# Attention and two feed-forward layers in one kernel: in blocks 3 and 4 a head pair's values stand behind the transposes of a later row

## The chip, the cores and the metric

The kernel runs on one core of a Trainium2 chip. A core has TensorE (PE in the profile, with its weight loads as PEld), VectorE (DVE), ScalarE (ACT), GpSimd (POOL) and SyncE (SP, which issues the DMAs). Each engine works through its own list of instructions in order; semaphores make one engine wait for another. The metric is the device time of one execution in microseconds (us); less is better.

## The reference

Windowed causal attention, followed by two feed-forward layers, all in float32:

```python
scores = scale * np.matmul(q, k.transpose(0, 1, 3, 2))       # B, H, S, D = 4, 8, 576, 64
mask = (rel >= 0) & (rel < window)                            # window = 128
scores = np.where(mask, scores + bias[None], -1000000000.0)
attn = np.exp(scores - np.max(scores, axis=-1, keepdims=True))
attn = attn / (np.sum(attn, axis=-1, keepdims=True) + 1e-09)
x = np.matmul(attn, v)                                        # to 2304 tokens x 512
h = x @ w_in; g = h * (1.0 / (1.0 + np.exp(-1.702 * h)))      # 512 -> 2048
x = g @ w_out                                                 # 2048 -> 512
g = x @ w_gate; val = x @ w_val                               # 512 -> 1536
out = (g * sigmoid(g) * val) @ w_out2                         # 1536 -> 512
```

## The kernel before

**Blocks.** The 2304 tokens are 18 tiles of 128, in five blocks of 4, 2, 4, 4 and 4 tiles (`A_BLOCKS`). Each block j goes through attention and then through the first feed-forward layer. That layer runs over 16 slices f of its hidden width. `h_part(j, f)` makes one slice: 12 products into one PSUM bank `hp` (each float32 product is made of three, high by high, high by low and low by high), then tanh on ACT into `th` (L719), a step on DVE that reads `hp` for the last time (L721), the high part `gh` on ACT (L727) and the low part `gl` on DVE (L729). `y_part(j, f)`, two slices later, adds the slice to the block's result: 12 products into four banks `y`. "Products" below means these.

**Attention beside it.** While block j-1 is in its feed-forward layer, block j's attention is worked off in small pieces between the products. A head pair has two halves, so eight of each of the first two pieces and four of the third make a block:

- S (`scores_and_norm`): q by k into two banks `sb`, one for each head of the pair. The 16 matmuls take the two banks in turn, beginning with the second head's; they work on quarters of the array (64x64). Then DVE and ACT make the softmax, and POOL scales it.
- T (`transposed`): four transposes on TensorE into one bank `pt` (L554), then `apart`: ACT copies `pt` into the tile `pf` (L585) and POOL cuts it in two (L587, L590). `pf` has one buffer: it is written anew when the values of the pair before have read it.
- V (`values_and_x`): 48 matmuls on quarters of the array, from `pf` and v into two banks `xb` (L388), then `take_x`: ACT copies the first bank into `half` (L675), DVE adds it to the second (L676), ACT takes the high part `xh` (L677) and DVE the low part `xl` (L669).

**What sets the order.** For blocks 3 and 4 the list `PLACES` says at which place of the feed-forward layer a piece is traced: place 2i stands behind `h_part` of slice i, place 2i+1 behind `y_part`. `tc.issue_after` on `marks["h"]` and `marks["y"]` keeps the pieces behind the products that were traced before them, and the same call in `three` keeps the next products behind the last S and V. Inside these limits a scheduler puts each engine's instructions in order when the kernel is built.

**PSUM.** All of this shares eight banks, handed out as they come free: four are held by `y`, so `hp`, `sb`, `pt` and `xb` share the other four. A tile gets a bank whose former owner has been read for the last time, and its first matmul waits for that read.

**Beside it.** ACT and DVE also prepare the weights of the second layer in these blocks (`prepare`, `fraction`, `halves`: the tiles `raw`, `cs`, `wa`, `wb`, lines L253 to L263 and L299), a few steps behind each `h_part` and each `y_part` (`PACE`).

Of the kernel before, what the change touches and what calls it, by code (L numbers as in the profile page):

```python
# [78 lines left out]

LENGTHS = {1: 8, 2: 18}  # L80

JOINED = 3, 4

PLACES = (
    "", "S0", "", "S1", "", "", "", "T0 S2", "", "T1 S3", "", "V0", "", "T2 S4", "", "T3 S5", "", "V1",
    "", "T4 S6", "", "T5 S7", "", "V2", "", "T6", "", "T7", "", "V3", "", "",
)

QUARTERS = 1, 2

# [7 lines left out]
def attention_two_ffn(ctx: ExitStack, tc: tile.TileContext, q, k, v, w_in, w_out, w_gate, w_val, w_out2, yscr, wscr, woscr, out):  # L98
# [41 lines left out]
    def bank(name):  # L140
        return ps.tile([P, 512], F32, tag="b", name=name)
# [174 lines left out]
    units, wides = {}, []  # L316

    def is_wide(j, g):

        return j == 0 and g == 0  # L320

    def blocks_of(i):
        return range(1 if i == 0 else 0, 2)

    def fill(t, n):

        for _ in range(n):
            nc.tensor.matmul(out=t[:, :P], lhsT=ident, rhs=ident, start=True, stop=True)

    def span(j):  # L330

        t0, n = a_blocks[j]
        return t0, n, 0 if kind(t0) == "first" else 1

    def load_pair(j, hp):

        t0, n, lead = span(j)
        qr = att.tile([P, TMAX * P], F32, tag="qr", name="qr", bufs=2)
        kr = att.tile([P, (TMAX + 1) * P], F32, tag="kr", name="kr", bufs=2)
        vr = att.tile([P, 2, TMAX + 1, D], F32, tag="vr", name="vr", bufs=2)  # L340
        rows = slice(hp * P, (hp + 1) * P)
        nc.sync.dma_start(out=qr[:, : n * P], in_=q[rows, t0 * P : (t0 + n) * P])
        nc.sync.dma_start(out=kr[:, : (n + lead) * P], in_=k[rows, (t0 - lead) * P : (t0 + n) * P])
        for e in range(2):
            nc.sync.dma_start(out=vr[:, e, : n + lead, :], in_=v[2 * hp + e, :, t0 - lead : t0 + n, :])
        units[j, hp] = {"q": qr, "k": kr, "v": [vr[:, e] for e in range(2)]}
# [32 lines left out]
    def tiles_of(j, g):  # L379

        return range(2 * g, min(2 * g + 2, a_blocks[j][1]))
# [113 lines left out]
    def reciprocals(j, hp, g):  # L495
        m = 2 * len(tiles_of(j, g))
        prob, stat = units[j, hp]["prob", g]
        nc.vector.tensor_scalar(out=stat[:, 2, :m], in0=stat[:, 1, :m], scalar1=1e-9, scalar2=None, op0=ALU.add)
        nc.vector.reciprocal(out=stat[:, 3, :m], in_=stat[:, 2, :m])  # L499
# [33 lines left out]
    def transposes(j, hp, g, fills=0):  # L533


        u = units[j, hp]
        tiles = tiles_of(j, g)
        m = len(tiles)
        prob = u.pop(("prob", g))[0]
        if is_wide(j, g):  # L540
            u["pt", g] = [bank("pt") for _ in range(2)]
            fill(u["pt", g][0], fills)
            for e in range(2):
                for i in tiles:
                    for b in blocks_of(i):
                        to = (2 * i + b) * P
                        nc.tensor.transpose(
                            out=u["pt", g][e][:, to : to + P], in_=prob[e][:, i, b * P : (b + 1) * P], identity=ident
                        )
        else:  # L550
            pt = bank("pt")
            fill(pt, fills)
            for x in range(2 * m):
                nc.tensor.transpose(out=pt[:, x * P : (x + 1) * P], in_=prob[:, x], identity=ident)  # L554
            u["pt", g] = pt
        if "pf" not in u:
            if j > 0:
                u["pf"] = att.tile([P, 4 * TMAX, P], F32, tag="pf", name="pf", bufs=1)
            else:
                u["pf"] = wpool.tile([P, 4 * TMAX, P], F32, tag=f"w{PFS + hp}", name="pf")  # L560

    def apart(j, hp, g, select):

        u = units[j, hp]
        m = len(tiles_of(j, g))
        pt = u["pt", g]
        if is_wide(j, g):
            lo = P * blocks_of(2 * g)[0]
            to = u["pf"][:, 8 * g + 4 * select : 8 * g + 4 * select + 4, :].rearrange("p x c -> p (x c)")
            if (hp, select) in COPY_ON_VECTOR:  # L570
                nc.vector.tensor_copy(out=to[:, lo:], in_=pt[select][:, lo : 4 * P])
            else:
                nc.scalar.activation(out=to[:, lo:], in_=pt[select][:, lo : 4 * P], func=AF.Copy)
            return
        before = u["pf"][:, 8 * g : 8 * g + 4 * m : 2, :]
        own = u["pf"][:, 8 * g + 1 : 8 * g + 4 * m : 2, :]
        src = pt[:, : 2 * m * P].rearrange("p (x c) -> p x c", c=P)

        if (j, hp, g) in ON_VECTOR:
            for out_, mask in ((own, keep), (before, drop)):  # L580
                nc.vector.tensor_tensor(
                    out=out_, in0=src, in1=mask.unsqueeze(1).to_broadcast([P, 2 * m, P]), op=ALU.mult
                )
        elif not select:
            nc.scalar.activation(out=own, in_=src, func=AF.Copy)  # L585
        else:
            nc.gpsimd.affine_select(  # L587
                out=before, in_=own, compare_op=ALU.is_gt, fill=0.0, base=0, pattern=[[0, 2 * m], [-1, P]], channel_multiplier=1
            )
            nc.gpsimd.affine_select(  # L590
                out=own, in_=own, compare_op=ALU.is_ge, fill=0.0, base=0, pattern=[[0, 2 * m], [1, P]], channel_multiplier=-1
            )
# [101 lines left out]
    begun = {}  # L694
# [264 lines left out]
    def scores_and_norm(*u):  # L959
        with tc.issue_after(marks["h"]), tc.issue_after(marks["y"]):  # L960
            scores(*u)
        for e in range(2):
            minima(*u, e)
            exponentials(*u, e)
        reciprocals(*u)
        normalise(*u)

    def transposed(*u):
        if u[0] in JOINED:
            with tc.issue_after(marks["h"]), tc.issue_after(marks["y"]):  # L970
                transposes(*u)
        else:
            transposes(*u)
        for select in range(2):
            apart(*u, select)

# [95 lines left out]
    def hooks(j, length):  # L1072

        ev = []

        G = (a_blocks[j][1] + 1) // 2
        step = 2 * length * SPREAD / (G * H // 2)
        at = 2 * (begin[j] - length)
        lag = TRANSPOSE_LAG if j != 2 else 6.5

        def start():
            load_pair(j, 0)
            load_pair(j, 1)

        if j > 1:
            ev.append((at - 1, start))
        if j in JOINED:
            for n, place in enumerate(PLACES):
                for what in place.split():
                    h = int(what[1:])  # L1090
                    if what[0] == "V":
                        ev.append((at + n, lambda h=h: values_and_x(j, h)))
                        continue
                    u = j, h // G, h % G
                    if what[0] == "T":
                        ev.append((at + n, lambda u=u: transposed(*u)))
                        continue
                    ev.append((at + n, lambda u=u: scores_and_norm(*u)))
                    if h % G == G - 1 and h // G + 2 < H // 2:
                        ev.append((at + n + 1, lambda h=h: load_pair(j, h // G + 2)))  # L1100
            return [(min(p, 2 * begin[j] - 1), e) for p, e in ev]
        begun, scored, valued = 0, 0, []
        for h in range(G * H // 2):
            u = j, h // G, h % G
            scored = max(at + step * h, scored + 1)
            for p in valued:
                if p <= scored < p + APART:
                    scored = p + APART
            ev.append((scored, lambda u=u: scores_and_norm(*u)))
            last = h % G == G - 1  # L1110
            if last and h // G + 2 < H // 2:
                ev.append((at + step * (h + LOAD_LAG), lambda h=h: load_pair(j, h // G + 2)))
            begun = max(begun, at + step * h + lag)
            ev.append((begun, lambda u=u: transposed(*u)))
            if last:
                begun = begun + step * (VALUES_LAG if j != 2 else 1.6)
                valued.append(begun)
                ev.append((begun, lambda u=u: values_and_x(*u[:2])))
        return [(min(p, 2 * begin[j] - 1), e) for p, e in ev]

    ev = []
    for j in range(1, na):
        ev += hooks(j, LENGTHS.get(j, NF1))
# [178 lines left out]
```

## Time and profile before

| | before |
|---|---|
| three timed runs, median (lowest to highest) | 896.36 us (894.97 to 897.86) |
| the profiled execution's own time | 894.27 us |
| its span, from first to last instruction | 892.6 us |
| busy: PE, PEld, DVE, ACT, POOL | 99%, 89%, 75%, 51%, 14% |
| granted TensorE clock over the span | 0.998 |

The profile is of one execution; its own time is 1.67 us more than its span. In a timeline row the first number is the start and the second the duration. Matmuls are pipelined, so a row's duration overlaps the next row: what a piece costs TensorE is read from the distance between starts.

### The profile page before, as it was taken

To read this page: it belongs to the slowest core of one execution; us is meant where nothing else is said; L and a number is where in the kernel's file an instruction comes from. 1 tells how busy PE (TensorE), PEld (TensorE's weight loads), DVE (VectorE), ACT (ScalarE), POOL (GpSimd) and SP (SyncE) were. 2 spreads that over 40 slices of the span, in tenths; PEclk is the share of its full clock that TensorE was granted. 3 is DMA by queue.
4 is the path that set the end of the run, shared out by engine and by line. 5 is a ranking of instruction groups with operands and counts; after the bars stand their busy time and mean duration, and the time that the engine had idled before them with its cause. 6 is when DMAs were issued, how large, how long until landed. Compare 5 with 4: busy or idle time off the path is not lost.

```text
span 892.6 us, 15625 instructions
## 1 busy us (share of the span) xinstructions
PE 883.8 (99%) x5556; PEld 792.8 (89%) x5556; DVE 672.0 (75%) x1707; ACT 455.7 (51%) x1065; POOL 121.7 (14%) x218
## 2 busy tenths in 40 slices
PE   8999999999999999999999999999999999999998
PEld 6787779997778777788888999999999999999998
DVE  8988847758886788776757486779866779766777
ACT  6866646646555566554445364335344345344331
POOL 6401424403242123210000000000000000000000
PEclk9999999999999999999999999999999999999999
DMA  9961214435565575556864587787887787887664
GB/s 324 385 258 30 72 57 147 142 119 188 186 208 179 205 244 200 199 184 217 272 246 170 180 310 264 252 310 263 285 289 258 254 309 269 288 296 256 252 217 142
DMA packets 71309, 199.20 MB, mean 223 GB/s; under 512 B 6720, under 2 KB 37952, under 8 KB 64320
## 3 DMA queue, kind: packets, MB, share of 16 engines
q1 hardware_dynamic: 71232, 198.21, 62.8%
q8 instruction: 44, 0.72, 0.3%
q14 instruction: 33, 0.27, 0.1%
HBM read 155.71 MB, written 42.47 MB: 222 GB/s over the span
## 4 chain that ended last, share of the span: by engine, by line
PE 93%; DVE 5%; POOL 1%; issue 1%; ACT 0%; DVEq 0%; POOLq 0%; ACTq 0%
PE sx L847 17%; PE ox L847 8%; PE sz L847 8%; PE y L684 7%; PE hp L684 7%; PE y L686 7%; PE y L685 7%; PE hp L685 7%; PE hp L686 7%; PE oz L847 4%; PE sy L847 4%; PE xb L388 2%; PE sb L388 2%; PE oy L847 2%; PE pt L554 1%; DVE cv L228 1%
## 5 line engine op out<-in xcount | busy, mean ns | idle before, releaser
L847 PE MATMUL sx<-ya,wg 128*128 128x384 f32 x864 | 172.4, 335 | 0.0
L847 PEld LDWEIGHTS sx<-ya,wg 128*128 128x128 f32 x864 | 151.9, 188 | 0.1
L684 PE MATMUL hp<-xh,wt 128*128 128x512 f32 (+1 forms) x320 | 121.2, 379 | 0.0
L684 PE MATMUL y<-gh,wt 128*128 128x512 f32 (+1 forms) x320 | 119.3, 376 | 0.0
L685 PE MATMUL hp<-xl,wt 128*128 128x512 f32 (+1 forms) x320 | 118.2, 369 | 0.5 <-DVE xl L669 0.4
L686 PE MATMUL y<-gh,wt 128*128 128x512 f32 (+1 forms) x320 | 117.9, 369 | 0.0
L686 PE MATMUL hp<-xh,wt 128*128 128x512 f32 (+1 forms) x320 | 117.9, 368 | 0.0
L685 PE MATMUL y<-gl,wt 128*128 128x512 f32 (+1 forms) x320 | 117.8, 368 | 0.0
L847 PE MATMUL ox<-p,wg 128*128 128x384 f32 x432 | 89.6, 337 | 0.0
L876 DVE TENSOR_TENSOR p<-th,p 128x384 fp32r<-128x384 f32 x126 | 68.2, 554 | 28.1 <-ACT p L875 27.4
L847 PE MATMUL sz<-ya,wg 128*128 128x384 f32 x432 | 88.8, 336 | 0.0
L729 DVE TENSOR_TENSOR gl<-th,gh 128x512 fp32r<-128x512 f32 (+1 forms) x80 | 52.3, 655 | 39.8 <-ACT gh L727 39.3
L875 ACT ACTIVATE p<-th 128x384 fp32r<-128x384 f32 x126 | 63.5, 521 | 36.3 <-DVE th L871 28.6
L509 POOL TENSOR_SCALAR prob<-prob,stat 128x128 f32<-128x128 f32 x112 | 56.8, 525 | 183.0 <-DVE stat L499 116.3
L847 PEld LDWEIGHTS ox<-p,wg 128*128 128x128 f32 x432 | 76.5, 188 | 0.0
L847 PEld LDWEIGHTS sz<-ya,wg 128*128 128x128 f32 x432 | 76.1, 188 | 0.1
L727 ACT ACTIVATE gh<-th 128x512 fp32r<-128x512 f32 (+1 forms) x80 | 46.9, 586 | 53.3 <-PE y L686 27.4
L882 ACT ACTIVATE th<-c 128x384 f32<-128x384 f32 x54 | 28.3, 525 | 86.9 <-DVE c L867 86.7
L684 PEld LDWEIGHTS y<-gh,wt 128*128 128x128 f32 x320 | 60.2, 188 | 13.7 <-issue 2.9
L684 PEld LDWEIGHTS hp<-xh,wt 128*128 128x128 f32 x320 | 60.1, 188 | 13.6 <-issue 2.7
L685 PEld LDWEIGHTS hp<-xl,wt 128*128 128x128 f32 x320 | 60.2, 188 | 10.7 <-DVE xl L669 1.5
L686 PEld LDWEIGHTS hp<-xh,wt 128*128 128x128 f32 x320 | 60.1, 188 | 10.5 <-DVE wt L238 0.2
(110 smaller groups left out, 1555.6 us busy)
## 6 DMA issues: line engine op xcount, KB each, us to landing
wg<-w_scratch SPq DMA_DIRECT2D x36, 1024.0 KB, 5.1
wg<-w_scratch SPq DMA_DIRECT2D x36, 768.0 KB, 5.0
wg<-wo_scratch SPq DMA_DIRECT2D x18, 1024.0 KB, 6.7
wg<-wo_scratch SPq DMA_DIRECT2D x18, 768.0 KB, 7.5
w_scratch<-wa SPq DMA_DIRECT2D x24, 512.0 KB, 2.7
w_scratch<-wb SPq DMA_DIRECT2D x24, 384.0 KB, 3.3
wraw<-in_moe_w_in SPq DMA_DIRECT2D x16, 512.0 KB, 9.1
wraw<-in_moe_w_out SPq DMA_DIRECT2D x16, 512.0 KB, 9.2
```

The lines of the kernel that those rows point to most:

```text
L228: nc.vector.scalar_tensor_tensor(out=made["c"], in0=made["c"], scalar=3, in1=low, op0=ALU.logical_shift_left, op1=ALU.bitwise_or)
L388: return matmul(**kw).ins
L509: nc.gpsimd.tensor_scalar(out=of[x], in0=of[x], scalar1=stat[:, 3, x : x + 1], scalar2=1.0, op0=ALU.mult, op1=ALU.mult,)
L684: nc.tensor.matmul(out=out_ap, lhsT=whi, rhs=xhi, start=start, stop=False)
L685: nc.tensor.matmul(out=out_ap, lhsT=whi, rhs=xlo, start=False, stop=False)
L686: marks[products] = nc.tensor.matmul(out=out_ap, lhsT=wlo, rhs=xhi, start=False, stop=stop).ins
L727: a = nc.scalar.activation(out=gh[:, :m], in_=th[:, :m], func=AF.Copy)
L729: d = nc.vector.tensor_tensor(out=gl[:, :m], in0=th[:, :m], in1=gh[:, :m].bitcast(F32), op=ALU.subtract)
L847: nc.tensor.matmul(out=bank_[:, :HT], lhsT=w[:, kk, at, a, :], rhs=p2[2 * (q // 2 - 1) + kk, i][:, b, :] if m == "O" else y2[q // NP2, i][ ...
L875: nc.scalar.activation(out=t[:, 0], in_=src, func=AF.Copy)
L876: nc.vector.tensor_tensor(out=t[:, 1], in0=src, in1=t[:, 0].bitcast(F32), op=ALU.subtract)
L882: nc.scalar.activation(out=th, in_=g, func=AF.Tanh, scale=0.5)
```

## The change

The list `PLACES` is written anew for blocks 3 and 4. S and T keep their places. Three of the four V of a block move: V of pair 0 from place 11 to 13, of pair 1 from 17 to 19, of pair 2 from 23 to 25, each behind the T that stands there and, at 13 and 19, ahead of the S that stands there. V of pair 3 stays at 29, alone. `transposed` is cut in two: the transposes come first, then V, then `selected` (the copies of `apart`), then S. `pf` is handed out in `apart` and no longer in `transposes`, since V must have read the old one.

```diff
-JOINED = 3, 4
-
-PLACES = (
-    "", "S0", "", "S1", "", "", "", "T0 S2", "", "T1 S3", "", "V0", "", "T2 S4", "", "T3 S5", "", "V1",
-    "", "T4 S6", "", "T5 S7", "", "V2", "", "T6", "", "T7", "", "V3", "", "",
-)
+PLACES = {
+    3: """
+    | S0 | | S1 | | | | T0 S2 | | T1 S3 | | | | T2 V0 S4 | | T3 S5 | | | | T4 V1 S6 | | T5 S7 | | | | T6 V2 | | T7 | | V3
+    """,
+}
+PLACES[4] = PLACES[3]
...
     def transposed(*u):
-        if u[0] in JOINED:
+        if u[0] in PLACES:
             with tc.issue_after(marks["h"]), tc.issue_after(marks["y"]):
                 transposes(*u)
         else:
             transposes(*u)
+
+    def selected(*u):
         for select in range(2):
             apart(*u, select)
...
-            for n, place in enumerate(PLACES):
+            for n, place in enumerate(PLACES[j].split("|")):
+                late = None
...
                     if what[0] == "T":
                         ev.append((at + n, lambda u=u: transposed(*u)))
+                        late = u
                         continue
+                    if late:
+                        ev.append((at + n, lambda u=late: selected(*u)))
+                        late = None
                     ev.append((at + n, lambda u=u: scores_and_norm(*u)))
```

What this makes of the order on TensorE, at V of pair 0 in block 3. The numbers behind a name are those of the buffer; `xb_2890` and `xb_2891` are the first and the second of V's banks before, `sb_2980` and `sb_2981` the banks of S4. First the order before, from V's end to the first matmuls of S4:

```order
L388 MATMUL xb_2890<-pf_2719,vr_2435 64x64
L684 MATMUL hp_2933<-xh_1826,wt_729 128x512 [waits DVE_49,PE_49]
...
L684 MATMUL y_2650<-gh_2774,wt_704 128x512 [waits Activation_49]
...
L554 MATMUL pt_2971<-ident_70,prob_2733 128x128 [waits DVE_49]
L554 MATMUL pt_2971<-ident_70,prob_2733 128x128 x3
L388 MATMUL sb_2981<-kr_2634,qr_2633 64x192 [waits DMAHW6_49,DMAHW5_49,Activation_49]
L388 MATMUL sb_2980<-kr_2634,qr_2633 64x192 [waits DVE_49]
```

24 products stand between V and S4. In the changed kernel the same place reads as follows; here V's banks are `xb_2943`, the first, and `xb_2944`, and `sb_2980` lies in the bank that `xb_2943` had:

```order
L554 MATMUL pt_2938<-ident_70,prob_2733 128x128 [waits DVE_49,PE_49,Pool_49]
L554 MATMUL pt_2938<-ident_70,prob_2733 128x128 [waits Pool_49] x3
L388 MATMUL xb_2944<-pf_2719,vr_2435 64x64 [waits DVE_49,DMAHW4_49,PE_49,Pool_49]
L388 MATMUL xb_2943<-pf_2719,vr_2435 64x128 [waits DVE_49]
...
L388 MATMUL xb_2943<-pf_2719,vr_2435 64x64
L388 MATMUL sb_2981<-kr_2634,qr_2633 64x192 [waits DMAHW6_49,DMAHW5_49,DVE_49]
L388 MATMUL sb_2980<-kr_2634,qr_2633 64x192 [waits Activation_49]
```

V stands between T2 and S4, and the second matmul of S4 waits for ACT: for the copy `half` of `xb_2943`. The same three pieces stand so at four places: T2 V0 S4 and T4 V1 S6, in both blocks.

On ACT, at V of pair 0 in block 4. Before, `half` stands right behind `gh` of the slice whose `hp` products stand right ahead of V:

```order
L719 ACTIVATE th_4102<-hp_4089 128x512 [waits PE_49]
L253 ACTIVATE cs_4086<-raw_4019 128x512 [waits DMAHW5_49,DMAHW4_49,DVE_49]
L727 ACTIVATE gh_4105<-th_4102 128x512 [waits DVE_49]
L675 ACTIVATE half_4164<-xb_4136 128x512 [waits PE_49,Pool_49]
L262 ACTIVATE wa_4169<-cs_4086 128x2x128 [waits DMAHW2_49,DVE_49,Activation_49]
```

In the changed kernel `half` is the last of a longer list at the same place:

```order
L727 ACTIVATE gh_4105<-th_4102 128x512 [waits DVE_49]
L719 ACTIVATE th_4155<-hp_4142 128x512 [waits PE_49]
L262 ACTIVATE wa_4136<-cs_4086 128x2x128 [waits DMAHW2_49,DVE_49,Activation_49]
L262 ACTIVATE wa_4136<-cs_4086 128x2x128 [waits DVE_49]
L727 ACTIVATE gh_4158<-th_4155 128x512 [waits PE_49]
L262 ACTIVATE wb_4162<-cs_4086 128x3x128 [waits DMAHW1_49,DVE_49]
L253 ACTIVATE cs_4166<-raw_4117 128x512 [waits DMAHW3_49,DMAHW2_49,DVE_49]
L675 ACTIVATE half_4215<-xb_4187 128x512 [waits PE_49,Pool_49]
L585 ACTIVATE pf_4220<-pt_4182 128x4x128 [waits Pool_49]
```

`gh_4158` waits for TensorE there: `gh` has two buffers, and the one it takes is read by the `y` products that stand ahead of T2. Of the list behind it, `wb` and `cs` stand ahead of `half`; `cs` waits for DVE.

## Rows read from the trace of the kernel before

**Rows 1.** Windows, blocks 3 and 4: length, busy us by engine, clock, DMA.

```profile
195.00:300.00 105.00, 105.00 (x743) 84.54 (x742) 81.58 (x262) 60.15 (x159) 30.94 (x48) 1.00 0.55 191
300.00:405.00 105.00, 105.00 (x730) 83.52 (x729) 84.78 (x277) 63.55 (x166) 26.86 (x48) 1.00 0.58 204
```

**Rows 2.** Waits of PE, whole span: total us, times, longest; first of five.

```profile
PE pt L328 <- POOL ident masks.py:199: 1.4, 1, 1.4
```

**Rows 3.** Timeline of PE, block 4, V of pair 1, alone between products.

```profile
353.98 0.39 PE L686 MATMUL y<-gh,wt 128*128 128x512 f32 x1
354.30 1.58 PE L388 MATMUL xb<-pf,vr 64*64 64x64 f32 x48
355.81 0.50 PE L684 MATMUL hp<-xh,wt 128*128 128x512 f32 x1
356.15 0.39 PE L685 MATMUL hp<-xl,wt 128*128 128x512 f32 x1
356.38 0.39 PE L686 MATMUL hp<-xh,wt 128*128 128x512 f32 x1
```

**Rows 4.** Timeline of PE, block 4, T3 and S5 between products.

```profile
347.23 0.60 PE L554 MATMUL pt<-ident,prob 128*128 128x128 f32 x4
347.76 0.88 PE L388 MATMUL sb<-kr,qr 64*64 64x192 f32 x16
348.57 0.50 PE L684 MATMUL y<-gh,wt 128*128 128x512 f32 x1
348.91 0.40 PE L684 MATMUL hp<-xh,wt 128*128 128x512 f32 x1
```

**Rows 5.** Timeline, block 2: V, T behind it, `half`, the addition.

```profile
174.88 1.47 PE L388 MATMUL xb<-pf,vr 64*64 64x128 f32 x48
...
176.28 0.66 PE L554 MATMUL pt<-ident,prob 128*128 128x128 f32 x4
...
176.46 0.60 ACT L675 ACTIVATE half<-xb 128x512 f32<-128x512 f32 x1 [1.03 <-PE xb L388]
...
177.09 0.70 DVE L676 TENSOR_TENSOR xb<-xb,half 128x512 f32<-128x512 f32 x1 [1.21 <-ACT half L675]
```

**Rows 6.** Timeline of PE, block 4, T6 alone between products.

```profile
382.76 0.60 PE L554 MATMUL pt<-ident,prob 128*128 128x128 f32 x4
383.11 0.48 PE L684 MATMUL hp<-xh,wt 128*128 128x512 f32 x1
383.43 0.39 PE L685 MATMUL hp<-xl,wt 128*128 128x512 f32 x1
```

**Rows 7.** Timeline of ACT and DVE at T3 of block 4.

```profile
347.43 0.63 ACT L727 ACTIVATE gh<-th 128x512 fp32r<-128x512 f32 x1 [0.37 <-PE y L686]
...
348.10 0.84 DVE L729 TENSOR_TENSOR gl<-th,gh 128x512 fp32r<-128x512 f32 x1 [0.59 <-ACT gh L727]
...
348.86 0.42 DVE L254 TENSOR_SCALAR raw<-raw 128x512 uint32<-128x512 uint32 x1
```

**Rows 8.** Timeline of ACT and DVE around `half` of V2, block 4.

```profile
378.59 0.69 DVE L256 SCALAR_TENSOR_TENSOR cs<-cs,raw 128x512 uint32<-128x512 uint32 x1
379.31 0.42 ACT L262 ACTIVATE wa<-cs 128x256 fp32r<-128x256 f32 x1 [1.33 <-DVE cs L256]
379.32 0.70 DVE L299 TENSOR_TENSOR cs<-cs 128x128 f32<-128x128 f32 x3
379.64 0.58 ACT L675 ACTIVATE half<-xb 128x512 f32<-128x512 f32 x1
379.93 0.42 DVE L263 TENSOR_TENSOR wa<-cs,wa 128x256 fp32r<-128x256 f32 x1
```

**Rows 9.** Timeline of ACT and DVE around `half` of V1, block 4.

```profile
357.37 0.55 DVE L263 TENSOR_TENSOR wb<-cs,wb 128x384 fp32r<-128x384 f32 x1
...
357.96 0.66 ACT L253 ACTIVATE cs<-raw 128x512 f32<-128x512 f32 x1 [1.71 <-DVE wb L263]
358.52 0.59 ACT L675 ACTIVATE half<-xb 128x512 f32<-128x512 f32 x1
```

More of the change, by code (lines that the diff above doesn't have):

```diff
@@ L555, in transposes, with apart @@
             u["pt", g] = pt
+    def apart(j, hp, g, select):
+        u = units[j, hp]
         if "pf" not in u:
@@ L560, in transposes @@
                 u["pf"] = wpool.tile([P, 4 * TMAX, P], F32, tag=f"w{PFS + hp}", name="pf")
-    def apart(j, hp, g, select):
-        u = units[j, hp]
         m = len(tiles_of(j, g))
@@ L1086, in hooks @@
             ev.append((at - 1, start))
-        if j in JOINED:
-            for n, place in enumerate(PLACES):
+        if j in PLACES:
+            for n, place in enumerate(PLACES[j].split("|")):
+                late = None
                 for what in place.split():
@@ L1100, in hooks @@
                         ev.append((at + n + 1, lambda h=h: load_pair(j, h // G + 2)))
+                if late:
+                    ev.append((at + n, lambda u=late: selected(*u)))
             return [(min(p, 2 * begin[j] - 1), e) for p, e in ev]
@@ L1113, in hooks @@
             begun = max(begun, at + step * h + lag)
-            ev.append((begun, lambda u=u: transposed(*u)))
+            ev.append((begun, lambda u=u: (transposed(*u), selected(*u))))
             if last:
```

## The prediction

> **What bounds the kernel now.** I read first the windows of the two stages that the change touches. TensorE is busy for 105.00 of 105.00 us in each of them, at full granted clock (1.00, so 2.4 GHz), while DVE is busy for 81.58 and 84.78 and ACT for 60.15 and 63.55 [rows 1]. Then the waits of TensorE over the whole span: the longest is 1.4 us, at the start of the program [rows 2], and as the windows are full, none falls into blocks 3 and 4. So there is no wait here for the change to remove. What it can win is time that TensorE spends on passing from one kind of matmul to another; what it can lose is any wait that it puts on TensorE, since nothing but TensorE sets the end there. From there I went to the timeline of TensorE, for the price of a piece between products, and to the timelines of ACT and DVE, for how fast V's results are taken out of PSUM.
>
> **What the change removes: passages.** Products start 0.23 us apart (356.15 to 356.38) [rows 3]. A V that stands alone starts 0.32 us after the last product ahead of it, 0.09 more than that pace; the next product starts 1.51 us after V (354.30 to 355.81); and the one behind comes 0.34 us later, 0.11 more [rows 3]. So V alone costs 0.09 + 1.51 + 0.11 = 1.71 us. T with S behind it costs 0.53 (T to S), 0.81 (S to the next product) and again 0.34 - 0.23 = 0.11: 1.45 us [rows 4]. Together 3.16 us.
>
> With V between them, T to V should cost the 0.53 of T to S, since V and S work on the same quarters. V to S has no row. The nearest is V with T behind it in block 2, with the same 48 matmuls, where T starts 1.40 us after V [rows 5]; I take 1.40. Above it lies the 1.51 of V to a product [rows 3]; below, nothing says that a passage between equal quarters is free, and if the 0.09 of entering quarters were the price of a passage, 1.31. The sum is 0.53 + 1.40 + 0.81 + 0.11 = 2.85 us, so a place of this kind wins 0.31 (0.20 to 0.40). There are four, two in each block: 1.24 us.
>
> The third V that moves stands behind T6 and ahead of products. T6 alone costs 0.35 to the next product and 0.32 - 0.23 = 0.09 behind it, 0.44 us [rows 6]; with V alone 2.15. Together they cost 0.53 + 1.51 + 0.11 = 2.15. It wins nothing.
>
> The Trainium skill ("TensorEngine Tiling (Array Packing)", section Key Properties) says that changing the tiling mode drains TensorE, and changing the tile within a mode does not. The trace agrees: the 0.09 and 0.11 stand at V's edges. By that rule alone the change would win its four passages, the 1.24 us above.
>
> No instruction is added or removed. S and T keep their places, so the loads that are issued behind S keep theirs in SP's queue; the fetches and stores of the weight preparation move by a few rows with it. The POOL cuts of a pair's `pf` have more time than before, since V comes two places later.
>
> **What the change adds: a wait on TensorE.** Ahead, V's banks had 24 products to be emptied in. Now S stands right behind V, and the bank of S's second matmul is the first of V's two banks, free only when ACT has copied `half` from it. S is in order on TensorE, and the next products must follow S, so everything behind stands. Without a wait S's second matmul would start at about 0.53 + 1.40 + 0.05 = 1.98 us after T's start (0.05 is S's 0.81 over 16 matmuls).
>
> The least that the wait can be: in block 2, with ACT idle, `half` starts 0.18 us after V's successor could start, and DVE, which waits for it, starts 0.63 us after `half` (176.46, 177.09) [rows 5]. That frees S at 0.53 + 1.40 + 0.18 + 0.63 = 2.74: a wait of 0.76 us, 3.0 for the four.
>
> But ACT will not be idle. In the changed order `half` stands behind `gh` of the last slice and steps of the weight preparation, and this `gh` waits for the end of the `y` products ahead of T, so the list can't be worked off earlier. The same wait shows now at T3 of block 4: `gh` starts 0.20 us after T, released by a `y` product; `gl` follows on DVE at 0.87, and DVE's next instruction at 1.63 after T's start (347.23, 347.43, 348.10, 348.86) [rows 4, 7]. From there I follow the changed order at each place, in us after T's start:
>
> - Block 3, V0: DVE's step on `cs` (L256) at 1.63; `wa` on ACT 0.72 later, 2.35; `half` 0.33 later, 2.68 [rows 8]; S is free 0.63 later, 3.31. Wait: 3.31 - 1.98 = 1.33.
> - Block 3, V1: the same to `wa`; three subtractions on DVE last 0.70 (3.05), a second `wa`, `half` 0.33 later (3.38) [rows 8], S free at 4.01. Wait: 2.03.
> - Block 4, V0: DVE has `raw` at 1.63, for 0.42 [rows 7]; then `wb`, with `cs` on ACT 0.59 behind its start (2.64) and `half` 0.56 behind that (3.20) [rows 9]; S free at 3.83. Wait: 1.85.
> - Block 4, V1: three subtractions (0.70) and a split of `wa` (0.42) on DVE from 1.63 on, 2.75; `wb`, then `half`, taken at the 0.33 of a `wa` (3.08) [rows 8]; S free at 3.71. Wait: 1.73.
>
> The four make 6.9 us. It can be more: these chains suppose that ACT reaches `gh` when `y` ends. Now `half` of V1 in block 4 starts 2.71 us after V's successor (355.81 to 358.52) [rows 3, 9]; with such a delay S would be free 2.71 + 0.63 = 3.34 us after V's end, a wait of about 3.3 at each place, 13 in all. I take 6.9, between 3.0 and 13, and nearer the lower end, because while TensorE stands ACT and DVE catch up.
>
> The Trainium skill ("Perfetto Trace Analysis", section Matmuls) says that independent groups of matmuls should go through different banks, so that the emptying of one lies beside the matmuls of the next. That speaks against this change: S takes the bank that V has just filled. The trace agrees as far as it goes, since with 24 products between the two TensorE waits nowhere in these blocks.
>
> **Where the stall goes.** Behind S, the next `hp` takes the bank of `pt`, whose copy follows `half` on ACT by one instruction, while 12 `y` products lie between: no second wait. The next T (T3, T5) waits for V's second bank, that is for the addition, `xh` and `xl`: about 0.7 us each (the addition's 0.70 [rows 5]), 2.1 with `half` done, and 24 products of 0.23, 5.5 us, stand between. Covered; if it weren't, it would cost what is missing from 5.5.
>
> **The sum.** -1.24 + 6.9 = +5.7 us on the profiled execution's own 894.27: 900.0 us. That execution lies 2.1 us below the median of the timed runs (896.36). The forecast for the median is 896.36 + 5.7 = 902.1, said as **902 us**.
>
> **The rivals.** A measurement of this kernel can tell about 0.3% from no change, 2.7 us.
>
> - *ACT is ready* (not slower). At all four places `half` follows V at once. Price: 4 x 0.76 - 1.24 = +1.8, 898.2 us, no change that can be told. It decides below an average wait of (2.7 + 1.24) / 4 = 0.98 us. For it: in block 2 `half` waits for V with ACT idle [rows 5]. Against it: the order on ACT, with `cs` or `wa` behind DVE ahead of `half`. Chance 0.16.
> - *Passages alone* (the bank is free in time, so that the wait does nothing and only the four passages count): 896.36 - 1.24 = 895.1, the same again. To be faster by 2.7 us, a place would have to win 0.67, twice what its edges cost now. Against it: S's second matmul reads the bank's release from ACT, and ACT cannot copy before V ends. Chance 0.04, of which 0.02 with a gain above 0.3%. (It is what the rule on modes in the Trainium skill's "TensorEngine Tiling (Array Packing)" would give by itself.)
> - *ACT is late*: tanh of the slice before is held up by the softmax of the last S, `gh` comes late, and each place waits as long as `half` is late now: 13 - 1.24, near +12, 908 us; half of that excess gives 905. For it: the 2.71 us [rows 3, 9]. Against it: that V had `half` behind a `cs` that waited for DVE by 1.71 us [rows 9], on which nobody waited; it is the worst row. Chance 0.14.
> - *The forecast*, waits of 1.0 to 2.4 us at the places, +2.7 to +8 in all: 899.1 to 904.4. Chance 0.66.
>
> So faster 0.02, within 0.3% 0.18, slower 0.80. The range that leaves out no more than 2 in 10 runs from the case where ACT is ready (898.2) to the middle of the case where it is late (906).
>
> **What would show it.** In the waits of TensorE a new row, S's matmul or its weight load (`sb` L388) released by ACT's `half` (L675), four times, near 7 us in all; windows of blocks 3 and 4 in which TensorE is no longer busy throughout; starts from V to S's first matmul near 1.40 us; `half` right behind `wa`, `wa`, `cs` and `wb` in the order of the four places; no wait at the next T; a stage from block 4's end on of the same length as before. The prediction is wrong if TensorE waits elsewhere, for instance at T for POOL or at V for `pf`, or if the four waits are below 1 us.

## The result and the profile after

The changed kernel takes 904.58 us (median of 6, 902.84 to 907.96), the kernel before 897.11 beside it (median of 6, 894.97 to 900.41): ratio 1.0082, 95% interval 1.0060 to 1.0104. By the medians it is slower by 7.5 us. (The ratios here and below are taken over all runs, and differ by up to 0.15% from the quotient of the two medians.) Forecast were 902.0, the range 898.2 to 906.0, and slower with 0.80. The profiled execution took 905.49 us, its span 903.8.

First the waits of TensorE over the whole span (total us, times, longest), which answer to [rows 2]:

```profile
PE sb L388 <- ACT half L675: 5.6, 4, 1.7
PE y L684 <- ACT gh L727: 1.9, 1, 1.9
...
PE y L685 <- DVE gl L729: 0.6, 1, 0.6
```

The first row is the one that the prediction named. The other two belong to one place behind block 4 and were not foreseen. The windows of blocks 3 and 4, against [rows 1]: TensorE is no longer busy throughout.

```profile
195.00:300.00 105.00, 102.60 (x733) 82.86 (x733) 77.82 (x255) 59.28 (x156) 24.12 (x48) 1.00 0.55 191
300.00:405.00 105.00, 101.81 (x716) 81.19 (x715) 82.68 (x272) 60.84 (x160) 25.34 (x48) 1.00 0.56 196
```

One of the four places, T2 V0 S4 of block 4, on the timelines of TensorE, ACT and DVE:

```profile
341.92 0.60 PE L554 MATMUL pt<-ident,prob 128*128 128x128 f32 x4
342.45 1.58 PE L388 MATMUL xb<-pf,vr 64*64 64x64 f32 x48
343.82 0.38 PE L388 MATMUL sb<-kr,qr 64*64 64x128 f32 x2
345.92 0.88 PE L388 MATMUL sb<-kr,qr 64*64 64x128 f32 x14 [1.73 <-ACT half L675]
346.73 0.50 PE L684 MATMUL y<-gh,wt 128*128 128x512 f32 x1
...
342.22 0.42 ACT L262 ACTIVATE wa<-cs 128x256 fp32r<-128x256 f32 x1 [1.07 <-DVE cs L299]
342.54 0.62 ACT L727 ACTIVATE gh<-th 128x512 fp32r<-128x512 f32 x1
343.06 0.51 ACT L262 ACTIVATE wb<-cs 128x384 fp32r<-128x384 f32 x1
344.72 0.66 ACT L253 ACTIVATE cs<-raw 128x512 f32<-128x512 f32 x1 [1.15 <-DVE wb L263]
345.28 0.59 ACT L675 ACTIVATE half<-xb 128x512 f32<-128x512 f32 x1
345.76 0.60 ACT L585 ACTIVATE pf<-pt 128x512 f32<-128x512 f32 x1
...
344.14 0.55 DVE L263 TENSOR_TENSOR wb<-cs,wb 128x384 fp32r<-128x384 f32 x1
```

S begins at 343.82, behind V, and could have gone on. ACT comes to `half` at 345.28 only: `cs` stands ahead of it and waits 1.15 us for DVE's `wb`. S stands from its first pair of rows at 343.82 to 345.92. (The 16 and 48 matmuls that are told of S and V are rows of the trace: the kernel issues 8 and 24, and each leaves two rows. So the pair is S's first matmul, and the second one waits.) At the four places this gap is 1.24, 2.12, 2.10 and 1.84 us, where the prediction took 0.05 as unstalled. (The row of waits counts 5.6, less than these gaps, since it begins where the pair's modelled duration ends.)

From the start of S0 in block 3 to the start of V3 in block 4 TensorE takes 204.50 us (196.67 to 401.17; before 198.83, 195.91 to 394.74): +5.7. The remaining 5.5 us of the span's growth lie outside, 0.8 ahead and 4.8 behind. Most of the latter is here, in block 4's own feed-forward layer:

```profile
466.19 0.84 ACT L783 ACTIVATE ya<-yr 128x768 fp32r<-128x768 f32 x1 [6.55 <-DMA yr<-y_scratch]
...
467.60 0.49 PE L684 MATMUL y<-gh,wt 128*128 128x512 f32 x1 [1.91 <-ACT gh L727]
468.68 0.70 PE L685 MATMUL y<-gl,wt 128*128 128x512 f32 x1 [0.58 <-DVE gl L729]
469.18 0.63 PE L686 MATMUL y<-gh,wt 128*128 128x512 f32 x1
469.60 0.63 PE L684 MATMUL y<-gh,wt 128*128 128x512 f32 x1
```

ACT stands 6.55 us for a read (`ya` is the first step of the second layer's input), `gh` stands behind it, TensorE waits for `gh` and `gl`, and then its products start 0.42 us apart instead of 0.23 for some 3 us. In the profile of before ACT stood 4.88 us for the same read and TensorE did not wait.

### The profile page after: what moved, and what is told of

Same layout as the page of the kernel before. It is cut to its first block, busy times and chain, and to the rows that moved or that the text cites. A ratio compares the mean times of both kernels' runs of the same rounds, so it can differ in the third digit from the quotient of the medians.

```text
span 903.8 us, 15620 instructions
## 1 busy us (share of the span) xinstructions
PE 885.8 (98%) x5556; PEld 794.1 (88%) x5556; DVE 672.1 (74%) x1707; ACT 456.4 (51%) x1065; POOL 113.4 (13%) x218
## 3 DMA queue, kind: packets, MB, share of 16 engines
q1 hardware_dynamic: 71232, 198.21, 62.0%
## 4 chain that ended last, share of the span: by engine, by line
PE 75%; DVE 9%; DMA 8%; ACT 4%; issue 2%; SPq 1%; DVEq 0%; POOL 0%; ACTq 0%; POOLq 0%
PE sx L847 17%; PE ox L847 8%; PE sz L847 8%; PE y L684 5%; PE hp L684 4%; PE y L685 4%; PE y L686 4%; PE hp L685 4%; PE hp L686 4%; PE oz L847 4%; PE sy L847 4%; DMA raw<-in_moe_w_out 2%; PE oy L847 2%; PE sb L388 2%; DMA raw<-in_moe_w_gate 1%
## 5 line engine op out<-in xcount | busy, mean ns | idle before, releaser
L684 PEld LDWEIGHTS y<-gh,wt 128*128 128x128 f32 x320 | 60.6, 189 | 17.6 <-issue 4.5
L509 POOL TENSOR_SCALAR prob<-prob,stat 128x128 f32<-128x128 f32 x112 | 49.4, 459 | 191.3 <-DVE stat L499 108.6
L684 PEld LDWEIGHTS hp<-xh,wt 128*128 128x128 f32 x320 | 60.1, 188 | 12.0 <-issue 1.6
L685 PEld LDWEIGHTS y<-gl,wt 128*128 128x128 f32 x320 | 60.6, 189 | 10.8 <-DVE gl L729 1.1
L686 PEld LDWEIGHTS y<-gh,wt 128*128 128x128 f32 x320 | 60.6, 189 | 10.4
```

Of the source, the lines that this page charges most:

```text
L509: nc.gpsimd.tensor_scalar(out=of[x], in0=of[x], scalar1=stat[:, 3, x : x + 1], scalar2=1.0, op0=ALU.mult, op1=ALU.mult,)
L684: nc.tensor.matmul(out=out_ap, lhsT=whi, rhs=xhi, start=start, stop=False)
L685: nc.tensor.matmul(out=out_ap, lhsT=whi, rhs=xlo, start=False, stop=False)
L686: marks[products] = nc.tensor.matmul(out=out_ap, lhsT=wlo, rhs=xhi, start=False, stop=stop).ins
```

## The experiments

Three theories were put to the test. **A**: S waits for the bank that V has just filled, `half` is late because of what stands ahead of it on ACT, and the passages win a little. **B**: the order itself, V two places later with longer lists on ACT and DVE, costs the time, whatever the bank. **C**: part of the difference is made at the read of `yr` behind block 4, in its strong form by the changed kernel alone, in its weak form in any of these kernels, now and then. A stretch below is always the time on TensorE from S0 of block 3 to V3 of block 4, and the rest what the span has behind V3 (before: 198.83 and 497.86 us). Both are read from the one profiled execution of a kernel; the time given for a kernel is the median of all its runs.

**The change in block 3 alone** (`only3`).

```diff
-PLACES[4] = PLACES[3]
+PLACES[4] = """
+    | S0 | | S1 | | | | T0 S2 | | T1 S3 | | V0 | | T2 S4 | | T3 S5 | | V1 | | T4 S6 | | T5 S7 | | V2 | | T6 | | T7 | | V3
+    """
```

> The change in block 3 alone; block 4 keeps the old list. Theory A (S stands because its second bank is the one that V has just filled, and is free only when ACT has copied half; less the passages won): block 3's two gaps between S's first pair and its other matmuls were 1.24 and 2.12 us in the changed kernel, its two passages win 0.34 each, so +2.7 us against the kernel before, about 900 us, ratio 1.003, with two waits of sb on half and none in block 4; block 4 as before, 105.0 us busy of 105. Theory B (the order itself costs the time, through later V and longer lists on ACT and DVE, not the bank): also about half, so this run does not part A from B. Theory C (a good part of the difference comes after block 4, from the reads of yr that ACT waited for near 455 us): if that follows from the changed order of blocks 3 and 4, some of its 3 to 5 us stays; if it comes and goes by itself, the time is +2.7 whatever that place shows.

898.84 us against 897.15, ratio 1.0013 (0.9990 to 1.0036). Two waits on `half`, 2.4 us in all, both in block 3. Stretch 201.75: +2.9, as A says; B says about the same here.

**S one place later** (`later`). The edit is made for both blocks.

```diff
-T2 V0 S4 | | T3 S5 | | | | T4 V1 S6 | | T5 S7
+T2 V0 | S4 | T3 S5 | | | | T4 V1 | S6 | T5 S7
```

> V as in the changed kernel, but S4 and S6 one place later in both blocks, so that 12 products of hp (2.8 us) stand between V and S. Theory A: the longest gap was 2.1 us behind V, so it is covered by 2.8 us of products; the passage from V to S is lost, the one from T to V stays; 0 us against the kernel before within 1 us, ratio 0.999 to 1.001, no wait of sb on half, or a short one. Theory B (the later V and the longer lists on ACT and DVE cost the time): still slower by 4 us or more, with TensorE waiting elsewhere. Theory C: the wait on yr near 455 us stays if it follows from the later V.

901.46 us, ratio 1.0046 (1.0023 to 1.0068): by the time alone a miss for A, and what B forecast. Theory A was right at three places of four: block 3 takes 91.97 us from S0 to V3, before 92.01. At the fourth, V1 of block 4, V started at 360.99, and still:

```profile
366.69 0.43 DVE L254 TENSOR_SCALAR raw<-raw 128x512 uint32<-128x512 uint32 x1 [2.82 <-DMA raw<-in_moe_w_out]
367.62 0.66 ACT L253 ACTIVATE cs<-raw 128x512 f32<-128x512 f32 x1 [3.58 <-DVE wb L263]
368.19 0.58 ACT L675 ACTIVATE half<-xb 128x512 f32<-128x512 f32 x1
...
368.82 2.04 PE L388 MATMUL sb<-kr,qr 64*64 64x128 f32 x16 [3.30 <-ACT half L675]
370.79 0.79 PE L684 MATMUL y<-gh,wt 128*128 128x512 f32 x1
```

A load of `raw` comes late, DVE stands for it 2.82 us ahead of `wb`, `cs` on ACT waits for `wb`, and `half`, which needs none of this, stands behind `cs`. S waits 3.30 us although 2.8 us of products lie between. S itself then lasts 1.97 us instead of 0.80, and the first products behind it run at the slow pace too. With these the stretch is 204.28, +5.5, all of it in block 4. So the distance of V and S is not all: what stands ahead of `half` decides.

**`half` copied twice** (`twice`).

```diff
-nc.scalar.activation(out=half, in_=x[0][:, :m], func=AF.Copy)
+for _ in range(2 if j > 2 else 1):
+    nc.scalar.activation(out=half, in_=x[0][:, :m], func=AF.Copy)
```

> The changed kernel with half copied twice by ACT in blocks 3 and 4 (the second copy writes the same values again). Theory A: V's first bank comes free one copy later, 0.5 to 0.6 us, at each of four places: +2.2 us over the changed kernel, about +9.5 us against the kernel before, ratio near 1.0105, the four waits of sb on half longer by 0.5 to 0.6 each, and no other wait of TensorE in blocks 3 and 4. Theory B: ACT has spare time, so one more copy of 0.5 us adds nothing that can be seen at these places beyond what the changed kernel has.

911.95 us, ratio 1.0151 (1.0119 to 1.0182): 7.4 more than the changed kernel, where 2.2 were expected. V's bank is held longer, so that S takes the bank of the transposes, whose copy stands behind the first `half`:

```profile
349.82 1.55 PE L388 MATMUL sb<-kr,qr 64*64 64x128 f32 x14 [2.69 <-ACT pf L585]
```

The stretch is 213.25, 8.8 above that of the changed kernel's profile. The four gaps are 1.99, 2.46, 3.07 and 2.55 us, 2.8 more than there, 0.7 on average: about one copy more on ACT, one copy more of waiting. B, by which the copy adds nothing, does not fit. Nearly all of the rest is the clock: behind three of the four gaps S and the products run at about half their pace (products 0.42 to 0.43 us apart instead of 0.23), for 3.6 to 6.2 us each, and that costs 5.9 us in all.

**The transposes' bank copied first** (`early`).

Shortened, and the two comments are not in the kernel:

```diff
+    # in apart, ahead of V: the copy into the tile that the probabilities had
+    nc.scalar.activation(out=u["pc", g][:, : 2 * m], in_=pt, func=AF.Copy)
...
-in_=own
+in_=own_from        # POOL cuts pf from that tile, behind V
```

> The changed kernel's order on TensorE (T V S without products between), but in blocks 3 and 4 ACT copies the transposes' bank right behind T, while V runs, into the tile that the probabilities had (they are used up by then), and POOL cuts pf from there after V. So the bank that is free first is that of the transposes, and S takes it in place of V's first. Theory A: the copy of the transposes ends at 1.3 to 1.9 us after T, S's second matmul could start at 1.95: waits of 0 to 0.5 us at a place, the passages' 0.34 each won: -1.4 to +0.6 us against the kernel before, ratio 0.9985 to 1.0005; no wait of sb on half. Theory B (order, not bank): slower by 4 us or more, as the changed kernel.

901.64 us, ratio 1.0039 (1.0016 to 1.0062), stretch 201.95: +3.1 instead of -1.4 to +0.6. By the time alone (+4.5) this is again what B forecast. No wait on `half`, and two short ones on the copy (0.48 and 0.36 us). But T5 of block 4 waited 0.74 for `xl`, and S7 behind it 0.61 for DVE: the last steps of V's way stand behind the preparation on DVE, which there waited 1.30 us for `raw`. The rest is 502.68, +4.8, with the waits of TensorE for `gh` (1.4) and `gl` (0.6) at the read of `yr` in it, as in the changed kernel. A held for the bank and was incomplete: the engines that empty it were still tied to the loads of the preparation. The next runs take that away.

**The preparation kept away from V** (`calm_mark`, and with the early copy `calm_early_mark`); the control is the kernel before with the same holding (`before_calm`, without the last edit, by which later steps stay behind `half`), and the changed kernel ran once more (`after_again`).

Shortened, with comments that are not in the kernel:

```diff
+    held = {...}        # the two places ahead of T2 V0 S4 and of T4 V1 S6
+    def paced(at, n):
+        if at in held:
+            saved[0] += n
+            return
+        more = min(saved[0], n / 2)
+        saved[0] -= more
+        advance(n + more)
...
-            advance(PACE[j])
+            paced(2 * idx, PACE[j])
...
+            if j in PLACES:
+                marks["x"] = copied        # half: later steps of the preparation stand behind it
```

> The changed kernel with the weight preparation held back at the two places ahead of each T V S and given back afterwards, and with its later steps kept behind half. On ACT half then stands right behind gh at all four places, with no cs, wa or wb between; on TensorE the order and the banks are those of the changed kernel. Theory A (S waits for half, and half is late because it stands behind steps of the preparation, which themselves wait for DVE or for a load): only the floor is left, S's second matmul about 0.8 us behind its first at each of four places; with 0.34 won by each passage that is 4 x (0.76 - 0.34) = +1.7 us against the kernel before, ratio near 1.002, and 5.5 us less than the changed kernel. Theory B (the later V and the longer way of its values cost the time, whatever stands on ACT): as the changed kernel, +7 us.

> The same, and besides ACT copies the bank of the transposes right behind gh, ahead of half, and S's second bank is that one. Theory A: the copy starts about 0.85 us after T and is done 0.6 us later, before V ends at 1.9: no wait at S, the four passages won, and the preparation no longer stands ahead of V's additions, so the wait that the early copy alone had at T5 of block 4 (for xl, 0.74 us, behind a load of raw that DVE waited for) is gone: -1.4 us against the kernel before, ratio 0.997 to 1.001. Theory B: +4 us or more.

> The kernel before with the preparation held back at the same places and given back in the same way, V where it was. A control for the two runs with the preparation held: by theory A it changes nothing on TensorE in blocks 3 and 4 (105.0 us busy of 105), 0 us within 1; if the holding itself costs or wins time, for instance by loads and stores that come later and meet the reads of yr near 455 us, this run shows how much.

> The changed kernel once more, for its ratio beside the others on one chip and for a second look at the place near 467 us. Theory A: ratio 1.008 again, the four waits of sb on half 5.6 us in all within 0.5, 204.5 us from S0 of block 3 to V3 of block 4. Theory C: if the wait of TensorE for gh (1.9 us) and the stretch at 0.42 us a product behind it, in which ACT had stood for the read of yr, belong to the changed kernel, they are there again; if they come and go, this look has another size or none.

| | us | ratio to before (896.86) | stretch | rest |
|---|---|---|---|---|
| `calm_mark` | 903.69 | 1.0065 (1.0041 to 1.0090) | 202.29 | 503.38 |
| `calm_early_mark` | 898.58 | 1.0010 (0.9994 to 1.0027) | 198.21 | 500.35 |
| `before_calm` | 900.82 | 1.0049 (1.0024 to 1.0073) | 199.45 | 503.22 |
| `after_again` | 904.78 | 1.0082 (1.0059 to 1.0105) | 207.02 | 500.31 |

By the time alone `calm_mark` missed (+6.8, not +1.7). The control shows why: holding the preparation back costs 4.0 us by itself, and the profile has it in the rest (+5.4), not in the stretch (+0.6). It is the read of `yr` again:

```profile
461.31 0.84 ACT L783 ACTIVATE ya<-yr 128x768 fp32r<-128x768 f32 x1 [6.17 <-DMA yr<-y_scratch]
...
462.73 0.51 PE L684 MATMUL y<-gh,wt 128*128 128x512 f32 x1 [1.77 <-ACT gh L727]
463.80 0.50 PE L685 MATMUL y<-gl,wt 128*128 128x512 f32 x1 [0.57 <-DVE gl L729]
```

Against the control `calm_mark` is 2.9 us slower and `calm_early_mark` 2.2 faster. Against the kernel before, `calm_early_mark` is 1.7 slower where 1.4 less was forecast, with the ratio in the range that was given. `after_again` repeats the four waits (6.2 us in all, stretch 2.5 us longer than the first time) and has the waits at the read of `yr` with another size (0.7 and 0.6 us). The timelines of TensorE and ACT in `calm_mark`, at T2 V0 S4 of block 4 again:

```profile
342.08 0.38 PE L388 MATMUL sb<-kr,qr 64*64 64x128 f32 x2
343.05 0.87 PE L388 MATMUL sb<-kr,qr 64*64 64x128 f32 x14 [0.60 <-ACT half L675]
...
340.38 0.63 ACT L729 ACTIVATE gh<-th 128x512 fp32r<-128x512 f32 x1 [1.69 <-PE y L688]
342.40 0.60 ACT L675 ACTIVATE half<-xb 128x512 f32<-128x512 f32 x1 [1.39 <-PE xb L388]
```

Now ACT waits for V, not S for ACT's list, and the gap is 0.97 us, the same at all four places: the floor, forecast as 0.05 + 0.76 = 0.81. The order on TensorE and the banks are those of the changed kernel, so what is gone from its gaps of 1.24 to 2.12 us was due to the preparation ahead of `half`. In `calm_early_mark` none of the four S waits. But with the preparation held, V3 of block 4 waits for POOL's cut of `pf`, which it does not in the changed kernel:

```profile
398.42 1.43 PE L388 MATMUL xb<-pf,vr 64*64 64x64 f32 x41 [0.92 <-POOL pf L590]
```

This is `calm_mark`; in `calm_early_mark` the wait is 0.69 us. The larger floor (0.6 us over the four places) and this wait make up most of what separates its stretch, +3.5, from the +1.7 forecast.

**The read of `yr` used a slice later**, in the kernel before, in the changed one, in `calm_early_mark`, and in `calm_mark` with S one place later as in `later`.

```diff
-        if j == na - 1 and f >= CLOSE:
+        if j == na - 1 and f >= CLOSE and f != CLOSE + 1:
             in_order(first)
```

> The kernel before with one edit behind block 4: the reads of yr are issued where they were, but the first step that uses them (ya on ACT) is traced a slice later, behind the next gh. In the profile of before, ACT stood 4.9 us for that read and TensorE did not wait. Theory C in its weak form (this wait comes and goes with the read in any kernel): the runs near 900 us go, the median falls by 1 to 2 us, to about 895.5, and the spread of the runs narrows. If the wait belongs to the changed kernel alone: same as before.

> The changed kernel with the same edit. Two looks at the changed kernel had TensorE waiting for gh and gl near 467 us for 2.5 and 1.5 us, with products at half the clock behind the first. Theory A alone (all of the difference is made in blocks 3 and 4): 2 to 4 us less than the changed kernel, about 901.5, and 5.7 to 7 us more than the kernel before with the same edit. Theory C in its strong form (part of the changed kernel's +7.4 is made at the read of yr, and only there): the difference to the kernel before with the same edit falls to 4 us or less.

> T V S without products between, the preparation held back at two places ahead and its later steps kept behind half, the transposes' bank copied first, and the read of yr used a slice later. In the run without the last edit TensorE waited at none of the four places, and lost about 2.5 us at the read of yr. Theory A: 0.6 us less than the kernel before with the same edit in blocks 3 and 4; about 895, ratio 0.997 to 1.000, the fastest of the kernels with T V S. Otherwise, if holding the preparation back costs time elsewhere than at the read of yr: 898 or more.

> V behind T at the later place, S one place behind it (12 products between), the preparation held back and its steps kept behind half, the read of yr used a slice later. S moved one place later alone still lost 3.7 us at one place of block 4, where half stood behind a cs that waited for a load of raw. Theory A: with no cs ahead of half, the 2.8 us of products cover the copy at all four places: no wait of sb on half, 105.0 of 105 us busy, 0 us against the kernel before with the same read, about 896. Theory B (V two places later is itself dear): +4 us or more.

| | us (lowest to highest) | ratio to before (896.95) | stretch | rest |
|---|---|---|---|---|
| `before_late` | 894.90 (894.19 to 896.04) | 0.9977 (0.9961 to 0.9993) | 199.23 | 499.12 |
| `after_late` | 902.48 (899.92 to 905.35) | 1.0063 (1.0041 to 1.0085) | 206.84 | 498.67 |
| `calm_early_late` | 895.34 (894.22 to 896.67) | 0.9983 (0.9971 to 0.9995) | 197.71 | 499.44 |
| `later_calm_late` | 895.61 (894.64 to 896.08) | 0.9979 (0.9964 to 0.9995) | 199.02 | 498.55 |

All four rests lie within 0.9 us; without the edit they ran from 497.9 to 503.4. The two kernels with the preparation held no longer pay for it in the rest. The kernel before gains 2.0 us from it (its runs beside spread from 894.17 to 901.38), the changed one 2.1 to 2.3. So the wait at that read belongs to both kernels, and the difference between them stays: 902.48 - 894.90 = 7.6 us, a little more than the 5.7 to 7 that A gave. C fell in its strong form; in its weak form it stands. B, as far as it puts the cost on the order itself, fell with the last two rows: T V S, and V at the later place with S behind 12 products, take 895.3 and 895.6 us once ACT and DVE are free for V's banks. What was right in it, the longer lists on ACT and DVE, is what A names ahead of `half`. At T2 V0 S4 of block 4 `calm_early_late` shows what the change alone does to TensorE:

```profile
338.15 0.60 PE L555 MATMUL pt<-ident,prob 128*128 128x128 f32 x4
338.68 1.58 PE L388 MATMUL xb<-pf,vr 64*64 64x64 f32 x48
340.05 0.86 PE L388 MATMUL sb<-kr,qr 64*64 64x128 f32 x16
340.84 0.50 PE L693 MATMUL y<-gh,wt 128*128 128x512 f32 x1
...
338.89 0.58 ACT L564 ACTIVATE prob<-pt 128x512 f32<-128x512 f32 x1
```

ACT copies the transposes' bank at 338.89, while V runs, and S starts in that bank 1.37 us after V without a gap. The best kernel is none of these, though: `before_late`, with V where it was, is as fast, within the spread of the runs.

## Why the prediction was right, and where its sizes were off

**What bounds the kernel.** Right: TensorE had no idle time, and the gaps put on it stand in the time.

**Passages.** 0.31 forecast for each T V S; the rows give 0.53 (T to V), 1.37 (V to S) and 0.80 to 0.81 (S to a product): 0.34 won, 1.36 in all against 1.24. V2 behind T6 wins nothing, as said. By the rule that a change of tiling mode drains TensorE (the Trainium skill, "TensorEngine Tiling (Array Packing)", section Key Properties) V beside S, in one mode, saves such changes. The trace agrees in sign, with the 0.34 us. `calm_early_late`, its stretch 1.1 us below that of before, shows about this gain alone (V3 of block 4 waits 0.31 us there).

**The wait.** Forecast 1.33, 2.03, 1.85, 1.73; measured as the gap less 0.05: 1.19, 2.07, 2.05, 1.79 in the profiled execution, 7.1 us in all against 6.9; 7.7 each in `after_again` and `after_late`. What made `half` late was named rightly: `wa`, `wa`, `cs` and `wb` stand ahead of it at the four places, each behind DVE. The chains began with DVE's step behind `gl`, and that held within 0.25 us: at V0 of block 4 `gh` started 0.62 us after T and not 0.20, since a `wa` ahead of it waited for DVE. The floor under each wait was 0.92 us (`calm_mark`), not 0.76. The rule of going through different banks (the Trainium skill, "Perfetto Trace Analysis", section Matmuls) speaks against the change, and the runs agree: 7.1 us of gaps with V's bank, none with another and ACT free.

**The sum.** -1.36 + 7.10 = +5.7, which is the stretch of the profiled execution (+5.67) and the number forecast. By medians the change costs 7.5 to 7.9. What is missing is a term of the sum, not the mechanism: in `after_again` and `after_late` the gap at V0 of block 4 (2.16 and 2.19 us) was followed by products at the lower level of the clock, which cost about 1.6 us in each, and the sum of their gaps is 0.6 larger. In `after_late`: 7.74 - 1.36 + 1.6 = 8.0, and its stretch is 8.0 above that of before. The prediction priced a wait by its length alone. Only two of three profiled executions of this order have that term; for the other runs only the granted clock over the whole span is on record. In `after_late` the one run with 1.000 took 899.92 us, 5.0 above the median of `before_late`, and the three with 0.998 took 901.47 to 902.53, which fits.

**The next T.** Covered, as forecast, in all three profiled executions of the changed order. In `early` it was not, where the additions stood behind a late load.

**The stage behind block 4 of the same length.** Wrong in the profiled execution (+4.8 us), right on average: the read of `yr` strikes both kernels. That execution of before, at 894.27, was one in which it cost nothing.

**The rivals.** "ACT is ready" needed waits below 0.98 us; `calm_mark` shows that this would take another order on ACT. "ACT is late" did not come. In `later` `half` was later still at one place, but not for the rival's reason: `gh` had started at 360.80, ahead of V, and the load of `raw` was late.

Left open: why `raw` comes late in block 4 (its issue follows the preparation's own pace on SP's queue, but no run separated that), and why holding the preparation back makes the read of `yr` late; that its 4 us arise there is shown by one profile and by the rests with the later use, not by a control with both.

## What to carry to other kernels

Putting two matmul groups side by side saves the passage between them, here 0.34 us, and gives up the time in which the first one's banks were emptied: look up which bank the second group gets, who frees it, and what stands ahead of that copy on its engine, in order, down to the loads. A copy that frees PSUM for TensorE must not stand behind work that waits for a DMA. And read more than one execution before the rest of a profile is put down to a change: a read that arrives just in time in one is late in the next.

## What the runs showed of the hardware that was not expected

After some gaps TensorE's products start 0.42 to 0.43 us apart instead of 0.23. The window over such a stretch in `after_late` (length, busy us by engine, granted clock, DMA) and its first rows:

```profile
346.50:350.00 3.50, 3.50 (x13) 2.67 (x9) 3.49 (x13) 0.70 (x2) 1.21 (x2) 0.55 0.58 173
```

```profile
345.86 0.87 PE L388 MATMUL sb<-kr,qr 64*64 64x128 f32 x14 [1.82 <-ACT half L675]
346.67 0.64 PE L684 MATMUL y<-gh,wt 128*128 128x512 f32 x1
347.10 0.63 PE L685 MATMUL y<-gl,wt 128*128 128x512 f32 x1
347.53 0.63 PE L686 MATMUL y<-gh,wt 128*128 128x512 f32 x1
```

The granted clock is 0.55 there, near the lower of the two levels (1.2 GHz), and TensorE is busy throughout, so a window's busy share does not show the loss. It came after gaps at S and after the waits at the read of `yr`. The same place with a gap of 2.10 us, in the first profile of the changed kernel, had none, and neither had V1 of block 4 with 2.14 us in `after_late`. Behind a gap at S such a stretch cost 1.6 to 2.8 us (`after_again`, `after_late`, `twice`).
